# Part of V in the Q/K padding, interleaved early loads and a 256-token first chunk in a four-layer attention/GLU kernel

## The chip, the cores and the metric

The kernel runs on one core of one Trainium2 chip. The metric is the device time of one execution in microseconds (us). The fast runs of one kernel spread by up to 1.5%; a run is called fast or slow by comparison with the others of the same kernel. All comparisons below are between fast runs. "Span" is the length of the profiled execution; it is about 1.8 us shorter than the time given for that same execution.

Names of engines: PE is TensorE (matmul), PEld its weight load, DVE is VectorE, ACT is ScalarE, POOL is GpSimd, SP is SyncE, which here only issues DMAs.

## The reference, cut to what matters

```python
# S = 2048 tokens, D = 448, H = 16 heads of Dh = 28, F = 1792, bf16
def _A_ref(x, wqkv, wo):                 # attention: 8 keys at distances 0, 2, ..., 14
    qkv = (x @ wqkv).reshape(B, S, 3, H, Dh) ...
    logits = einsum(q, gathered k) * Dh ** -0.5    # masked, softmax over the 8 keys
    return einsum(attn, gathered v).reshape(B, S, D) @ wo

def _B_ref(x, w_gate, w_up, w_down):     # bilinear feed-forward
    return ((x @ w_gate) * (x @ w_up)) @ w_down

x = x + _A_ref(_layernorm(x), A_wqkv, A_wo)
x = x + _B_ref(_layernorm(x), B_w_gate, B_w_up, B_w_down)
x = x + _A_ref(_layernorm(x), ...)       # the same weights again
x = x + _B_ref(_layernorm(x), ...)
```

The four layers are numbered 0 to 3. Layers 0 and 2 are attention, 1 and 3 feed-forward.

## The kernel before: the parts that matter

A list scheduler, run in Python while the kernel is built, puts every operation into a fixed order on each engine. Layers overlap by chunks of 512 tokens. In attention, a head of 28 columns is stored in a slot of 32, so that Q and K carry four unused columns for each head.

Layernorm output is transposed before it feeds the matmuls. In layer 0 that is done on PE for the chunks in `PE_T`, and by a DMA transpose issued from SP for the rest. One chunk is four blocks of 128 tokens, so PE transposes blocks 0 to 11 and DMA blocks 12 to 15:

```python
PE_T = ("00","01","02")
# ... (in the layernorm of chunk j of layer li)
if not by_pe:
    sc.add("sp", one(lambda E, ...: E.dma_start_transpose(X[:, :, c0:c0 + 128], xn_sb[:, slot, 0:128 * nt]), ("T", li, B)), ...)
else:
    ... # E.transpose on PE into PSUM, then a copy by ACT or DVE
```

The loads: x and the V weights are issued from SP and the Q/K weights from ACT. The feed-forward weights are issued from ACT, one DMA each, only after the last quarter of x has landed. Gate weights go to partitions 0 to 63 and up weights to 64 to 127, because each pair of 64-row matmuls takes one operand half from each; the two run at the same time (fourteen of 512 columns, 376 ns each in the trace, take 1.69 us together). Down weights go to all 128 partitions:

```python
GATE = [("x", -1, 15)] if "02" in PE_T else [("xn", 0, 11)]
for nm, lo, src in (("wg", 0, B_w_gate), ("wu", 64, B_w_up)):
    plain_dma("act", WGU[lo:lo + 64, :, :], src.rearrange("(k p) f -> p k f", p=64), nm, f"d_{nm}", deps=GATE, ...)
plain_dma("act", WD[:], B_w_down.rearrange("(c p) e -> p c e", p=128), "wd", "d_wd", deps=GATE, ...)
```

The V matmuls of a pair of query blocks are 448 columns wide (the query blocks are 120 tokens, in groups of two):

```python
nv = D // 2 if split else D
def rhs(which, dc, lo, hi):
    return WV[lo:hi, dc, nv * which:nv * which + nv] if split else WV[lo:hi, dc, :]
```

The softmax here doesn't subtract the row's maximum and nothing guards it: scores larger than these inputs give would overflow.

Of the kernel before, what the change touches and what calls it, by code (L numbers as in the profile page):

```python
# [5 lines left out]
dt = mybir.dt  # L6
# [3 lines left out]
S = 2048  # L10
# [17 lines left out]
PE_T = ("00","01","02")  # L28
HEAD_LN = 4
HEAD_P = (-30.0,-29.5,-19.3,-17.8)  # L30
HOLD_A = 0.0
HOLD_BA = 2000.0
HOLD_BB = 0.0
HOLD_N = 2
# [5 lines left out]
LN0 = (2,2)  # L40
LN1 = (2,2)
VFIRST = False
WARM = 18
FILL = 30
SEED = 0
JITTER = 0.0
ATT_P = 0.6
A_CAP = 6
B_CAP = 8
SEQ = "A00 A01 B10 A02 B11 A03 B12 A20 B13 A21 B30 A22 B31 A23 B32 B33".split()  # L50
# [30 lines left out]
class Sched:  # L81
# [13 lines left out]
    def add(self, engs, ins, est, deps=(), prio=0.0, mode=None, acquire=None, release=(), dma=None, lat=0.0, after=None, selfd=()):  # L95
# [7 lines left out]
        op.prio += JITTER * self.rng.random()  # L103
        self.ops.append(op)
# [37 lines left out]
    def pick_banks(self, req, now):  # L142
        ok = [self.holder[b] is None and self.free_at[b] + self.LAT <= now + 1e-6 for b in range(8)]
        if req.pair:
            pairs = [p for p in range(4) if ok[2 * p] and ok[2 * p + 1]]
            if len(pairs) < req.n // 2:
                return None
            pairs.sort(key=lambda p: max(self.free_at[2 * p], self.free_at[2 * p + 1]))
            got = []
            for p in pairs[:req.n // 2]:  # L150
                got += [2 * p, 2 * p + 1]
            return got
        cand = [b for b in range(8) if ok[b]]
        if len(cand) < req.n:
            return None
        cand.sort(key=lambda b: (ok[b ^ 1], self.free_at[b]))
        return cand[:req.n]

    def schedule(self):
        self.holder = [None] * 8  # L160
        self.free_at = [-1e9] * 8
        self.last_rel = [None] * 8
# [24 lines left out]
        while left:  # L187
            moved = False
            b_ready = any(o.acquire is not None and o.acquire.kind == 1 for o in pend["pe"])
            for e in self.ENGS:  # L190
# [11 lines left out]
                for *_, op in cands:  # L202
                    if op.acquire is not None:
# [5 lines left out]
                        cap = (A_CAP if b_ready else 8) if kind == 0 else (B_CAP if a_wait else 8)  # L209
# [159 lines left out]
def build(nc, A_x, A_wqkv, A_wo, B_w_gate, B_w_up, B_w_down, out):  # L369
# [11 lines left out]
    NXN, NV, NE, NR, NG = 6, 4, 3, 3, 4  # L381
# [14 lines left out]
    v_sb = sb([128, NV, 512], bf, "v_sb")  # L396
    E_sb = sb([128, NE, 4, EW], bf, "E_sb")
    R_sb = sb([128, NR, EW], dt.float32, "R_sb")
    g_sb = sb([128, NG, 512], bf, "g_sb")
    hT = sb([128, FC, 2, 512], bf, "hT")  # L400
    oT = sb([128, 4, HALF], bf, "oT")
    ones32 = sb([128, 32], bf, "ones32")
    MK = sb([128, 3, 128], bf, "MK")
    ident = sb([128, 128], bf, "ident")
    warm = sb([128, 256], bf, "warm")
# [5 lines left out]
    sem_names += [f"d_x{i}" for i in range(NCH)] + ["d_stg0", "d_stg1", "d_stg2", "d_stg3", "d_wv", "d_wo", "d_wg", "d_wu", "d_wd", "d_out", "d_out2"]  # L411
    sem_names += [f"d_t{p}_{j}" for p in range(2) for j in range(NCH)]
# [14 lines left out]
    def load_x(q):  # L427
        two, b0 = q // 2, 4 * (q % 2)
        plain_dma("sp", x_sb[:, 4 * q:4 * q + 4, :], x_par[two][:, b0:b0 + 4, :], [("x", -1, B) for B in range(4 * q, 4 * q + 4)],
                  f"d_x{q}", lat=3300.0 + 700.0 * q, prio=-50 + q)  # L430

    load_x(0)
    for c in range(4):
        plain_dma("sp", WV[:, c, :], A_wqkv[CH_ROWS[c]:CH_ROWS[c] + 128, 2 * D:3 * D], ("wv", c), "d_wv", lat=5000.0, prio=-49.9)
    for q in range(1, NCH):
        load_x(q)
    for c in range(4):
        plain_dma("act", stage[:, 2 * D * c:2 * D * (c + 1)], A_wqkv[CH_ROWS[c]:CH_ROWS[c] + 128, 0:2 * D], ("stg", c), f"d_stg{c}", lat=4300.0, prio=-60)
# [5 lines left out]
    memset("dve", warm[:], 0.0, "c_warm", 100)  # L444
# [5 lines left out]
    sc.add("pool", one(lambda E: E.memset(v_sb[:].rearrange("p s (h e) -> p (s h) e", e=32)[:, :, DH:32], 1.0), "c_v"), 400, prio=-40)  # L450
    memset("pool", MK[:], 1.0, "i_mk0", 300)
# [10 lines left out]
    for n in range(WARM + FILL):  # L462
        sc.add("pe", one(lambda E: E.matmul(ps[:, wb[0], 0:256], warm[:, 0:128], warm[:], start=True, stop=True), ("warm", n)), 214.0 if n < WARM else 109.0, deps=["c_warm"], mode="F",
# [9 lines left out]
    WQKR = [("wqk", c, w) for c in range(4) for w in range(2)]  # L473
    WVR = [("wv", c) for c in range(4)]
    for j in range(4):
        dst = wo_g[32 * j:32 * j + DH, :, :]
        src = A_wo.rearrange("(c j e) d -> j e c d", c=4, j=4, e=DH)[j]
        plain_dma("sp", dst, src, ("wo", j), "d_wo", deps=["c_wo"], lat=12000.0, prio=-45)
    GATE = [("x", -1, 15)] if "02" in PE_T else [("xn", 0, 11)]
    for nm, lo, src in (("wg", 0, B_w_gate), ("wu", 64, B_w_up)):  # L480
        plain_dma("act", WGU[lo:lo + 64, :, :], src.rearrange("(k p) f -> p k f", p=64), nm, f"d_{nm}", deps=GATE, lat=12000.0 if lo == 0 else 20000.0, prio=-44)
    plain_dma("act", WD[:], B_w_down.rearrange("(c p) e -> p c e", p=128), "wd", "d_wd", deps=GATE, lat=26000.0, prio=-43)
    WO = [("wo", j) for j in range(4)]

    rings = {n: [None] * k for n, k in (("xn", NXN), ("v", NV), ("e", NE), ("r", NR), ("g", NG))}
# [17 lines left out]
    def ln_chunk(li, j, prio):  # L503
# [3 lines left out]
        groups = LN0 if li == 0 and j == 0 else LN1  # L507
        B0 = 4 * j
# [10 lines left out]
        for B in range(4 * j, 4 * j + 4):  # L519
# [6 lines left out]
            else:  # L526
                src = _twice_view(x_sb[:, B, :])
                dst = xn_sb[:, slot, :].rearrange("p (a t n) -> p a t n", a=7, t=2)
                c0 = 512 * (nbs[(li, j)] % 2) + 128 * (B % 4)
# [4 lines left out]
            if not by_pe:  # L534
                sc.add("sp", one(lambda E, slot=slot, c0=c0: E.dma_start_transpose(X[:, :, c0:c0 + 128], xn_sb[:, slot, 0:128 * nt]), ("T", li, B)),
                       1300.0, deps=[("xn", li, B)] + war, dma=f"d_t{par}_{j}", mode=li, lat=1400.0 if par == 0 else 1900.0, prio=prio)
# [18 lines left out]
    def crossed(parts, deps, prio, est, acquire):  # L555
        prev, prevk = None, []
        for n, (half, ins, pdeps) in enumerate(parts):
# [13 lines left out]
    def twin(u, tdeps, prio):  # L571
# [8 lines left out]
        crossed(parts, u["deps"] + tdeps, prio, pe_cols(u["n"]), u["bk"])  # L580

    def twin_blocks(outs, lhs, rhs, keys, groups, gdeps, deps, prio, acquire):
# [13 lines left out]
        crossed(parts, deps, prio, pe_cols(D), acquire)  # L596

    def qk_chunk(li, j, prio):
        X = xnT[0]
        c0 = 512 * j  # L600
        tdeps = [("T", li, B) for B in range(4 * j, 4 * j + 4)]
        war = []
        if li >= 2:
            lo, hi = 512 * j, 512 * (j + 1)
            for qb in range(NQB):
                k0, nk, tok, nq = qb_info(qb)
                if k0 < hi and tok + nq > lo:
                    war.append(("S", li - 2, qb))

        def unit(c):  # L610
            bk = Banks(2, pair=True)
            def out(which):
                return ps[:, bk[which], :]
            def lhs(which, dc, lo, hi):
                return WQK[lo:hi, dc, 1 - which, 128 * c:128 * c + 128]
            def rhs(which, dc, lo, hi):
                return X[lo:hi, dc, c0:c0 + 512]
            return dict(bk=bk, out=out, lhs=lhs, rhs=rhs, n=512, deps=WQKR, keys=(("Kps", li, j, c), ("Qps", li, j, c)), c=c)

# [3 lines left out]
        for u in us:  # L623
            bk, c = u["bk"], u["c"]
            def mk(eng, bk=bk, c=c):
                dst = qk[:, :, c, c0:c0 + 512]
                def fn(E):
                    src = ps[:, bk[0]:bk[0] + 2, :]
                    return E.activation(dst, src, ACT.Copy) if hasattr(E, "activation") else E.tensor_copy(dst, src)  # L629
                return fn  # L630
            sc.add(("act", "dve"), one(mk(None), ("QK", li, j, c)), {"act": act_est(1024), "dve": dve_est(1024)},
                   deps=[("Kps", li, j, c), ("Qps", li, j, c)] + war, release=[(bk, 0), (bk, 1)], prio=prio)
        for B in range(4 * j, 4 * j + 4):
            readersA.setdefault((li, B), []).extend([("Kps", li, j, 3), ("Qps", li, j, 3)])

    vslot = {}

    def v_group(li, qbs, prio):
# [15 lines left out]
        split = len(qbs) == 1  # L654
        nv = D // 2 if split else D
# [6 lines left out]
        def rhs(which, dc, lo, hi):  # L662
            return WV[lo:hi, dc, nv * which:nv * which + nv] if split else WV[lo:hi, dc, :]
        keys = tuple(("Vps", li, qbs[0], w) for w in range(2)) if split else tuple(("Vps", li, q) for q in qbs)
        twin(dict(bk=bk, out=out, lhs=lhs, rhs=rhs, n=nv, deps=WVR, keys=keys), tdeps, prio)
        n = len(qbs)
        s0 = slots[0][0]
        nk = infos[0][1]
        def fn(E):
# [3 lines left out]
            else:  # L673
                dst = v_sb[0:nk, s0:s0 + n, :].rearrange("p s (h e) -> p s h e", e=32)[:, :, :, 0:DH]
                src = ps[0:nk, bk[0]:bk[0] + n, 0:D].rearrange("p s (h e) -> p s h e", e=DH)
            return E.activation(dst, src, ACT.Copy) if hasattr(E, "activation") else E.tensor_copy(dst, src)  # L676
        sc.add(("act", "dve"), one(fn, [("V", li, q) for q in qbs]), {"act": act_est(n * D), "dve": dve_est(n * D)},
               deps=list(keys) + [p for _, p in slots] + ["c_v"], release=[(bk, 0), (bk, 1)], prio=prio)
# [3 lines left out]
    def attn_front(li, qb, prio):  # L682
# [3 lines left out]
        jl = ck // 512  # L686
        jh = (tok + nq - 1) // 512
        deps = [("QK", li, j, c) for j in range(jl, jh + 1) for c in range(4)]
# [25 lines left out]
    def attn_back(li, qb, slot, prio):  # L714
# [5 lines left out]
        for b in range(4):  # L720
            if not by_pe:
                break
            ins.append((lambda E, b=b: E.matmul(ps[32 * b:32 * b + 32, bk[1], 0:4 * nq], ones32[0:nk, :], E_sb[0:nk, slot, b, 0:4 * nq], start=True, stop=True, tile_position=(0, 32 * b)),
                        ("Dn", li, qb) if b == 3 else None))
        for h in range(H):
            b, hc = h % 4, h // 4
            ins.append((lambda E, b=b, hc=hc, h=h: E.matmul(ps[32 * b:32 * b + 32, bk[0], hc * nq:hc * nq + nq], v_sb[0:nk, vs, 32 * h:32 * h + 32],  # L727
                                                            E_sb[0:nk, slot, b, hc * nq:hc * nq + nq], start=True, stop=True, tile_position=(0, 32 * b)),
                        ("AV", li, qb) if h == H - 1 else None))
        sc.add("pe", ins, (200.0 if by_pe else 0.0) + 4 * 54.0, deps=[("E", li, qb, 0), ("E", li, qb, 1), ("V", li, qb), "c_ones", "c_v"], mode="C32", acquire=bk, prio=prio)  # L730
# [4 lines left out]
        else:  # L735
            sc.add("dve", one(lambda E: E.stream_shuffle(R_sb[:, rs, 0:4 * nq], ps[:, bk[0], 0:4 * nq], [DH] * 32), ("Rs", li, qb)), dve_est(4 * nq) + 100.0,  # L736
                   deps=[("AV", li, qb), prev], prio=prio)
# [5 lines left out]
        for B in range(tok // 128, (tok + nq - 1) // 128 + 1):  # L743
            if B >= 8:
                war.append(("Y", li, B - 8))
            elif li >= 2:
                war.append(("Y", li - 2, B + 8))
        cut = [tok] + [HALF] * (tok < HALF < tok + nq) + [tok + nq]
        ins = []
        for a, z in zip(cut, cut[1:]):  # L750
            def fn(E, a=a, z=z):
                return E.tensor_tensor(oT[:, :, a % HALF:a % HALF + z - a], ps[:, bk[0], 0:4 * nq].rearrange("p (h n) -> p h n", h=4)[:, :, a - tok:z - tok],  # L752
                                       R_sb[:, rs, 0:4 * nq].rearrange("p (h n) -> p h n", h=4)[:, :, a - tok:z - tok], ALU.mult)
            ins.append((fn, ("N", li, qb) if z == cut[-1] else None))
        sc.add("dve", ins, dve_est(4 * nq, fixed=70.0 * len(ins)), deps=[("AV", li, qb), ("R", li, qb)] + war, release=[(bk, 0)], prio=prio)
# [23 lines left out]
    def b_chunk(li, j, n_b, prio):  # L779
# [3 lines left out]
        tdeps = [("T", li, B) for B in range(4 * j, 4 * j + 4)]  # L783

        def unit(fc):
            acq = Banks(2, kind=1)
            def out(which):
                return ps[:, acq[which], :]
# [164 lines left out]
```

## Time and profile before

| | before |
|---|---|
| time, median of 4 | 409.46 us (three runs at 409.09 to 409.69; the fourth, 423.57, was slow and is not used) |
| span of the profiled run | 409.2 us (an execution of about 411.0 us, so slower than the median) |
| PE / DVE / ACT busy | 97% / 69% / 51% |
| first Q/K matmul, first gate/up matmul | 10.86 us, 68.74 us |
| PE work ordered before the first gate/up matmul (worked out as said below) | 43.1 us |

The first part of the page gives each engine's busy time, share of the span and number of instructions:

```profile
PE 395.4 (97%) x4606; PEld 191.3 (47%) x4606; DVE 281.8 (69%) x556; ACT 210.5 (51%) x356; POOL 11.9 (3%) x23
```

97% on PE looks as if only less matmul work could help. But busy is not the same as useful. A pair of 64-row matmuls takes columns/2.4 plus about 2.6 ns, by the starts in the timeline (from one group's start to the next, four pairs of 224 columns take 0.38 us at 111.81 us and seven pairs of 512 take 1.51 us at 87.36 us); summed over the instruction order that makes 367.5 us. The other 42 us lie mostly before 100 us. The table of busy time by stretch shows where (columns: the stretch, busy us and instruction count of each engine, granted PE clock, share of the 16 DMA engines, GB/s; a share over 1 means overlapping packets):

```profile
core 0: us, PE busy (x) PEld busy (x) DVE busy (x) ACT busy (x) POOL busy (x), PEclk, DMA share, GB/s
10.00:20.00 10.00, 7.86 (x64) 3.81 (x64) 7.14 (x22) 3.93 (x10) 0.00 (x0) 0.84 0.96 214
20.00:30.00 10.00, 9.70 (x122) 4.34 (x120) 7.92 (x19) 8.36 (x16) 2.12 (x1) 0.99 1.04 200
30.00:40.00 10.00, 8.97 (x154) 4.04 (x154) 7.29 (x14) 9.08 (x15) 2.09 (x1) 1.00 1.27 206
40.00:50.00 10.00, 8.83 (x126) 3.96 (x124) 9.52 (x16) 5.73 (x9) 2.00 (x1) 1.00 0.01 2
60.00:80.00 20.00, 17.48 (x216) 7.43 (x216) 17.12 (x36) 12.45 (x24) 0.00 (x0) 0.91 0.26 42
```

PE has holes and a lowered clock in 10 to 20 us and 60 to 80 us. And the DMA engines are full from 10 to 40 us at only about 200 GB/s: that is the feed-forward weights. The first hole has its origin on ACT. This is ACT's timeline (start, us, instruction, and in brackets the idle time before it):

```profile
12.23 0.70 ACTq L422 DMA_DIRECT2D WGU<-in_B_w_gate_dram  x1
12.96 1.51 ACTq L422 DMA_DIRECT2D WGU<-in_B_w_up_dram  x1
14.51 0.68 ACTq L422 DMA_DIRECT2D WD<-in_B_w_down_dram  x1
15.23 0.30 ACT L514 ACTIVATE lnv<-mv,eps_sb 128x2 f32<-128x2 f32 x1 [4.68 <-issue]
```

ACT's queue stands at the weight DMAs until x has landed (12.2 us), then spends 3 us issuing them. The layernorm step behind them finds ACT idle for 4.68 us; its own input from DVE was done at about 12.45 us, so the step comes some 2.8 us late. PE pays in its timeline:

```profile
10.86 3.85 PE L578 MATMUL ps<-xnTa,WQK 64*128 64x512 bf16 x34
16.82 1.01 PE L541 MATMUL ps<-ident,xn_sb 128*128 128x128 bf16 x8 [2.12 <-DVE mv L513]
17.76 2.90 PE L578 MATMUL ps<-xnTa,WQK 64*128 64x512 bf16 x14
```

Fourteen matmuls then take 2.90 us, where at full clock fourteen of the same take 1.69: the granted clock was 0.50 from 17 to 20 us.

The V group and the four DMA transposes of layer 0, in SP's timeline, with the line that gives their time from issue to landing:

```profile
L578 PE MATMUL ps<-WV,xnTa 64*128 64x448 bf16 (+1 forms) x252 | 28.5, 351 | 0.7 <-ACT E_sb L703 0.4
...
30.20 8.54 SPq L535 DMA_TRANSPOSE xnTa<-xn_sb  x4
...
DMA to landing us min/median/max: 3.5/5.8/7.8
```

Transposes of the later layers mostly land in about 2.5 to 3 us.

### The profile page before, as it was taken

What the parts mean: (1) busy time and instruction counts of PE and PEld (TensorE: products, weight loads), DVE (VectorE), ACT (ScalarE), POOL (GpSimd) and SP (SyncE); (2) the same over time, 40 slices, a digit from 0 to 9 for tenths busy, and PEclk for the clock granted to TensorE, in tenths of its full rate; (3) what the DMA queues carried; (4) which work ended last, traced back from release to release, by engine and by line L of the source; (5) the groups of instructions that cost most, each with busy time, mean ns of one, the idle gap of its engine ahead of it and who ended that gap; (6) DMA issues with size and microseconds to landing.
All of it is one profiled execution on the core that took longest, in us unless ns stands there. A gap on an engine that the chain in (4) does not pass through costs nothing.

```text
span 409.2 us, 10575 instructions
## 1 busy us (share of the span) xinstructions
PE 395.4 (97%) x4606; PEld 191.3 (47%) x4606; DVE 281.8 (69%) x556; ACT 210.5 (51%) x356; POOL 11.9 (3%) x23
## 2 busy tenths in 40 slices
PE   8798897999999999999999999999999999999997
PEld 6344333444544454444544445444554444444444
DVE  5687987989597768966697778964789723433432
ACT  4488586575368554667536584344854321321420
POOL 5022100000000000000000000000000000000000
PEclk9899998999999999999999999999999999999999
DMA  8999112430231033200241002310232032001001
GB/s 283 208 203 186 25 24 46 37 56 9 40 72 27 2 47 47 53 2 0 48 68 32 0 4 46 72 26 2 47 39 55 2 72 67 2 2 45 2 2 45
DMA packets 49573, 20.90 MB, mean 51 GB/s; under 512 B 41400, under 2 KB 48632, under 8 KB 49528
## 3 DMA queue, kind: packets, MB, share of 16 engines
q1 hardware_dynamic: 46072, 14.44, 19.1%
q10 hardware_dynamic: 3456, 5.79, 6.1%
q8 instruction: 36, 0.59, 0.6%
q14 instruction: 9, 0.07, 0.1%
HBM read 8.43 MB, written 1.84 MB: 25 GB/s over the span
## 4 chain that ended last, share of the span: by engine, by line
PE 89%; DVE 4%; ACT 2%; DMA 2%; SPq 1%; issue 1%; ACTq 1%
PE ps L797 41%; PE ps L594 25%; PE ps L578 16%; PE ps L727 2%; PE ps L696 2%; DMA x_sb<-in_A_x_dram 2%; PE ps L818 1%; DVE E_sb L709 1%; DVE qk L629 1%; ACT E_sb L703 1%; SPq L422 1%; ACTq L422 1%; DVE hT L806 1%; DVE x_sb L770 1%; PE ps L541 1%
## 5 line engine op out<-in xcount | busy, mean ns | idle before, releaser
L797 PE MATMUL ps<-xnTb,WGU 64*128 64x512 bf16 x1568 | 176.2, 376 | 1.6 <-DVE hT L806 0.4
L803 ACT ACTIVATE g_sb<-ps 128x512 bf16<-128x512 f32 x112 | 66.7, 598 | 108.4 <-PE ps L797 107.4
L797 PEld LDWEIGHTS ps<-xnTb,WGU 64*128 64x128 bf16 x1568 | 76.4, 94 | 89.6 <-issue 3.0
L806 DVE TENSOR_TENSOR hT<-g_sb,ps 128x512 bf16<-128x512 bf16 x112 | 75.6, 682 | 43.1 <-ACT g_sb L803 42.0
L594 PE MATMUL ps<-WD,hT 64*128 64x448 bf16 x840 | 85.0, 349 | 0.9 <-DVE hT L806 0.6
L703 ACT ACTIVATE E_sb<-ps 128x960 bf16<-128x960 f32 (+1 forms) x68 | 63.8, 972 | 16.0 <-PE ps L696 15.1
L594 PEld LDWEIGHTS ps<-WD,hT 64*128 64x128 bf16 x840 | 41.2, 94 | 38.7 <-DVE hT L806 1.2
L770 DVE TENSOR_TENSOR x_sb<-x_sb,ps 128x448 bf16<-128x448 bf16 x62 | 35.9, 614 | 33.5 <-PE ps L594 33.2
L578 PE MATMUL ps<-xnTa,WQK 64*128 64x512 bf16 x448 | 54.8, 383 | 0.4 <-ACT v_sb L676 0.2
L709 DVE TENSOR_TENSOR E_sb<-E_sb,MK 128x960 bf16<-128x960 bf16 (+1 forms) x65 | 43.5, 679 | 12.0 <-ACT E_sb L703 11.2
L511 DVE BATCH_NORM_STATS2 st<-x_sb 128x6 f32<-128x448 bf16 x64 | 37.2, 613 | 3.2 <-DMA x_sb<-in_A_x_dram 3.1
L532 DVE TENSOR_SCALAR xn_sb<-x_sb,mv,rstd 128x512 bf16<-128x512 bf16 (+1 forms) x64 | 34.1, 573 | 3.1 <-ACT rstd L516 2.9
L578 PEld LDWEIGHTS ps<-xnTa,WQK 64*128 64x128 bf16 x448 | 20.9, 95 | 26.4 <-issue 1.6
L629 ACT ACTIVATE qk<-ps 128x1024 bf16<-128x1024 f32 x22 | 22.4, 1023 | 20.7 <-PE ps L578 20.6
L594 PE MATMUL ps<-wo_g,oT 64*128 64x448 bf16 x256 | 29.7, 350 | 0.2
L578 PE MATMUL ps<-WV,xnTa 64*128 64x448 bf16 (+1 forms) x252 | 28.5, 351 | 0.7 <-ACT E_sb L703 0.4
L752 DVE TENSOR_TENSOR oT<-ps,R_sb 128x480 bf16<-128x480 f32 (+3 forms) x36 | 22.3, 625 | 4.1 <-ACT R_sb L740 3.8
L738 ACT ACTIVATE R_sb<-R_sb 128x480 f32<-128x480 f32 (+1 forms) x30 | 18.0, 600 | 13.4 <-DVE R_sb L736 13.3
L740 ACT ACTIVATE R_sb<-R_sb 128x480 f32<-128x480 f32 (+1 forms) x34 | 20.6, 606 | 0.3
L736 DVE STREAM_SHUFFLE R_sb<-ps 128x480 f32<-128x480 f32 (+1 forms) x30 | 20.6, 694 | 0.0
L629 DVE CAST qk<-ps 128x1024 bf16<-128x1024 f32 x10 | 12.2, 1225 | 9.3 <-PE ps L578 9.3
L594 PEld LDWEIGHTS ps<-wo_g,oT 64*128 64x128 bf16 x256 | 12.3, 95 | 12.5 <-PE ps L594 1.1
(47 smaller groups left out, 156.3 us busy)
## 6 DMA issues: line engine op xcount, KB each, us to landing
x_sb<-in_A_x_dram SPq DMA_DIRECT2D x4, 448.0 KB, 6.5
out_dram<-x_sb SPq DMA_DIRECT2D x15, 112.0 KB, 1.7
WGU<-in_B_w_gate_dram ACTq DMA_DIRECT2D x1, 1568.0 KB, 11.0
WGU<-in_B_w_up_dram ACTq DMA_DIRECT2D x1, 1568.0 KB, 18.2
WD<-in_B_w_down_dram ACTq DMA_DIRECT2D x1, 1568.0 KB, 22.8
hT<-in_A_wqkv_dram ACTq DMA_DIRECT2D x4, 224.0 KB, 4.9
xnTb<-xn_sb SPq DMA_TRANSPOSE x32, 3.0
WV<-in_A_wqkv_dram SPq DMA_DIRECT2D x4, 112.0 KB, 5.4
```

What stands on the lines that cost most here:

```text
L511: sc.add("dve", one(lambda E, B=B: E.bn_stats(st6[:, B, :], x_sb[:, B, :]), ("bn", li, B)), 525.0, deps=[("x", li - 1, B)] + ([("xn", li - ...
L532: sc.add("dve", one(lambda E, B=B, dst=dst, src=src: E.tensor_scalar(dst, src, mv[:, B, 0:1], rstd[:, B:B + 1], ALU.subtract, ALU.mult), ( ...
L578: parts[0 if s < 3 else 1][1].append((lambda E, w=w, c=c, lo=lo, st=st, sp_=sp_: E.matmul(u["out"](w), u["lhs"](w, c, lo, lo + 64), u["rhs ...
L594: ins.append((lambda E, w=w, c=c, lo=lo, st=st, sp_=sp_: E.matmul(outs(w), lhs(w, c, lo), rhs(w, c, lo), start=st, stop=sp_), keys[w] if s ...
L629: return E.activation(dst, src, ACT.Copy) if hasattr(E, "activation") else E.tensor_copy(dst, src)
L703: return E.activation(E_sb[0:nk, slot, 2 * hp:2 * hp + 2, 0:4 * nq], ps[0:nk, b0:b0 + 2, 0:4 * nq], ACT.Exp, scale=SCALE)
L709: return E.tensor_tensor(e, e, m, ALU.mult)
L752: return E.tensor_tensor(oT[:, :, a % HALF:a % HALF + z - a], ps[:, bk[0], 0:4 * nq].rearrange("p (h n) -> p h n", h=4)[:, :, a - tok:z - ...
L770: sc.add("dve", one(lambda E: E.tensor_tensor(x_sb[:, B, :], x_sb[:, B, :], ps[:, bk[w], 0:D], ALU.add), ("x", li, B)), dve_est(D), deps=[ ...
L797: ins.append((lambda E, u=u, k=k, w=w: E.matmul(u["out"](w), WGU[64 * w:64 * w + 64, k, 128 * u["fc"]:128 * u["fc"] + 128], X[64 * w:64 * ...
L803: sc.add("act", one(lambda E, gs=gs, bk=bk: E.activation(g_sb[:, gs, :], ps[:, bk[0], :], ACT.Copy), ("G", li, j, fc)), act_est(512), deps ...
L806: sc.add("dve", one(lambda E, gs=gs, bk=bk, fc=fc: E.tensor_tensor(hT[:, fc, hs, :], g_sb[:, gs, :], ps[:, bk[1], :], ALU.mult), ("H", li, ...
```

## The change

The intent is to take work off PE and to shorten the start:

- V of 4 of the 16 heads is computed in the unused Q/K columns, stored to DRAM and brought back by DMA transposes. The V matmuls shrink from 448 to 336 columns, except for the first four query blocks of layer 0.
- x comes in halves and quarters, the Q/K weights are split over both queues, the gate weights come in four column pieces, two of them issued by ACT at the very start. Up weights go to SP, down weights to ACT in two pieces.
- The first chunk of tokens is 256 instead of 512 (chunks 256/512/512/512/256 in layers 0, 1 and 3).
- Attention output is copied out of PSUM before it is normalised (`AVC`). The scheduler's priorities are new.

The diff, cut to its core:

```diff
 PE_T = ('00', '01', '02')
+VT = 4
+AVC = True
+PLAIN = 4
+ACH = {0: (256, 512, 512, 512, 256), 2: (512, 512, 512, 512)}
+BCH = {1: (256, 512, 512, 512, 256), 3: (256, 512, 512, 512, 256)}
 ...
-GATE = [("x", -1, 15)] if "02" in PE_T else [("xn", 0, 11)]
-for nm, lo, src in (("wg", 0, B_w_gate), ("wu", 64, B_w_up)):
-    plain_dma("act", WGU[lo:lo + 64, :, :], ..., nm, f"d_{nm}", deps=GATE, ...)
-plain_dma("act", WD[:], ..., "wd", "d_wd", deps=GATE, ...)
+plain_dma("sp", WGU[64:128, :, :], B_w_up..., "wu", "d_wu", ...)
+for n in range(4):
+    plain_dma("act", WGU[0:64, :, f0:f1], B_w_gate[:, f0:f1]..., ("wg", n), f"d_wg{n}", deps=[("rstd", 0, 3)] * (n > 1), ...)
+for n in range(2):
+    plain_dma("act", WD[:, 7 * n:7 * n + 7, :], ..., ("wd", n), f"d_wd{n}", deps=[("rstd", 0, 7)], ...)
 ...
+# after each Q/K chunk: 7 small stores of the padding columns to DRAM ("PW");
+# for each query block: sc.add("sp", ... dma_start_transpose(v2_sb[:, slot, :], vt_dram[li][:, k0:k0 + 128]) ("VT")
 ...
-nv = D // 2 if split else D
+nv = VD // 2 if split else D if plain else VD      # VD = 448 - 4 * 28 = 336
```

`PE_T` has not changed, but its chunks have. Three chunks now cover blocks 0 to 9 instead of 0 to 11.

## The prediction

> **What bounds the kernel.** TensorE (PE). The page gives PE 97% busy, DVE 69%, ACT 51%; the chain that ended last is 89% PE. From matmul starts in the timeline a pair of 64-row matmuls costs columns/2.4 + about 2.6 ns (eight 224-column ones take 0.38 us, so the slope holds). Summing the instruction order so gives 367.5 us of pure matmul work in 409.2 us. The other 42 us: nothing useful before the first transpose at 9.0 us (8.1 busy us there are warm-up), about 10 us of idle PE after it, nearly all before 70 us (2.1 at 15-17, 1.0 at 33, 1.2 at 43-44, 2.0 at 62-64), about 3.4 us lost at half clock (granted clock 0.50 in 17-20 us and around 65-68 us, each just after an idle stretch), 2.4 us after the last matmul, and the rest is 123 changes of array tiling at about 0.13 us. [...]
>
> **What the change does.**
> 1. V of 4 of 16 heads rides in the Q/K padding: V matmuls shrink from 448 to 336 columns for 30 of 34 query blocks. 105 pairs x 112/2.4 ns = 4.9 us less PE work, all critical. Price: 56 small DMAs to DRAM and 30 DMA transposes back, on SP. Transposes now land 2.5-3.0 us after issue, out-stores 1.7 us, so this V should come 7-10 us after its Q/K copy; mostly hidden.
> 2. Head. x in halves, Q/K weights split over both queues, 256-token first chunk. The last Q/K weight still lands near 8 us, but two blocks need less layernorm. First Q/K matmul about 9 us instead of 10.9. The gate-weight DMAs no longer sit in the middle of ACT's stream: now they hold ACT from 10.6 to 15.2 us, starve the layernorm and cause both the 2.1 us hole and the half clock after it. Worth 4-5 us.
> 3. First gate/up matmuls move from 43 us to 37 us of preceding PE work, filling holes where DVE (about 80-95% busy before 70 us) is the limit: 1-3 us.
> 4. Costs: AV copies out of PSUM, 30 x about 0.55 us on ACT/DVE, off the chain but releasing banks sooner; 256-column chunks +0.6 us PE; 6 more tiling changes +0.8 us; last chunk's final H awaited by all remaining matmuls, +0.8 us.
>
> Sum: 409.5 - 4.9 - 0.4 (fewer transposes) + 2.2 - 6.5 = about 400.
>
> **Prediction: 400 us, 8 in 10 between 395 and 405.5.** Faster by over 2%: 0.63; within 2%: 0.36; slower: 0.01.
>
> **What would show it.** V matmul group: busy 28.5 to about 23 us, 336-column pairs near 143 ns. First Q/K matmul at or before 9.5 us. PE idle between 9 and 70 us down from about 9 to under 5 us, no 0.50 clock at 17-20 us. First gate/up matmul at 50-56 us, not 68.7. Waits of the AV matmuls on v transposes under 1 us in total. DVE busy about 290, ACT about 220 us. After 100 us, PE idle stays about 2.5 us.
>
> **What would make it wrong.** Weights queued on SP ahead of transposes could delay the first DMA transposes to 35 us and stall the fourth chunk; gate pieces loaded early may delay x and starve the layernorm; the DRAM round trip may be longer than planned, holding AV and in-order SP behind it; new idle gaps may drop the clock again at another place.

The sum comes to 409.5 - 4.9 - 0.4 + 2.2 - 6.5 = 399.9, about 400 us; the 3.4 us at half clock are read from the trace (a mean clock of 0.992 over 409.2 us makes 3.3 us). The 0.13 us for a change of array tiling is an estimate, since the prediction puts down to 123 changes what is left of the 42 us. In the timeline of the kernel before a change adds about 0.10 us: seven pairs of 512 columns take 1.61 us with a change behind them (81.19 to 82.80 us) and 1.51 us without (87.36 to 88.87 us).

## The result, and the profile after

| | before | after |
|---|---|---|
| time, median of 4 | 409.46 us | 405.78 us (405.61 to 406.66) |
| ratio, 95% interval | | 0.9896 (0.9865 to 0.9926): the same within 2% |
| span of the profiled run | 409.2 us | 404.0 us |
| first Q/K matmul | 10.86 us | 10.83 us |
| first gate/up matmul | 68.74 us | 60.61 us |
| PE work ordered before it | 43.1 us | 36.7 us |
| time not covered by PE work, first 100 us | 27.3 us | 26.4 us |

Ratios here and below are the mean time of one kernel's fast runs over that of the other's of the same rounds, so they are not quite the ratio of the medians that are quoted. Where I turn a ratio into us, I multiply by 410 us. The last two rows are worked out as before, from columns and instruction order. The profiled run of the kernel before was slower than its median, so the spans (5.2 us apart) show more than the medians (3.7 us).

PE is less busy, by 7 us, and the V group shrank as planned. But the first gate/up matmul came 8.1 us earlier with 6.4 us less PE work ahead of it, so the start itself gained hardly 2 us, and over the first 100 us only 1 us. First the busy line and the V group of the kernel after:

```profile
PE 388.4 (96%) x5046; PEld 211.9 (52%) x5046; DVE 293.1 (73%) x602; ACT 222.6 (55%) x406; POOL 15.8 (4%) x29
...
L650 PE MATMUL ps<-WV,xnTa 64*128 64x336 bf16 (+2 forms) x252 | 22.8, 301 | 0.1
```

The waits of PE in the first 100 us (releaser, us in total, times, longest):

```profile
PE ps L650 <- DMA xnTa<-xn_sb: 4.7, 1, 4.7
PE ps L612 <- DVE xn_sb L603: 2.6, 2, 1.6
PE ps L907 <- DVE R_sb L842: 1.2, 1, 1.2
```

The longest is new, a wait on a DMA transpose. Here it is in PE's timeline, with SP's two groups of transposes and the time to landing below:

```profile
34.40 1.69 PE L650 MATMUL ps<-xnTa,WQK 64*128 64x512 bf16 x14
40.82 1.47 PE L650 MATMUL ps<-xnTa,WQK 64*128 64x512 bf16 x6 [4.73 <-DMA xnTa<-xn_sb]
...
26.45 8.12 SPq L606 DMA_TRANSPOSE xnTa<-xn_sb  x4
35.15 4.39 SPq L606 DMA_TRANSPOSE xnTa<-xn_sb  x2
...
DMA to landing us min/median/max: 3.9/8.9/12.0
```

The stretches, to be set against those of before:

```profile
10.00:20.00 10.00, 8.29 (x123) 5.13 (x122) 7.65 (x26) 7.11 (x15) 1.21 (x6) 1.00 1.13 266
20.00:30.00 10.00, 9.91 (x144) 4.72 (x140) 9.44 (x24) 8.65 (x19) 4.28 (x2) 1.00 1.07 222
30.00:40.00 10.00, 6.08 (x82) 2.43 (x76) 7.83 (x7) 5.67 (x8) 4.00 (x2) 0.95 1.22 202
40.00:50.00 10.00, 9.18 (x98) 3.99 (x100) 3.54 (x5) 3.77 (x6) 0.00 (x0) 0.70 0.27 49
50.00:60.00 10.00, 9.46 (x180) 5.44 (x176) 9.24 (x19) 7.33 (x12) 0.00 (x0) 1.00 0.48 57
60.00:80.00 20.00, 19.10 (x334) 14.64 (x336) 18.45 (x43) 14.79 (x34) 0.00 (x0) 1.00 0.23 46
```

The hole and the half clock have moved from 15 to 20 us and 62 to 68 us, to 36 to 46 us. PE shows 9.18 busy in 40 to 50 us, but at a mean clock of 0.70. The pieces of the chain that ended last, in order of time, name the two early limits:

```profile
2.81 9.32 DMA x_sb<-in_A_x_dram
...
32.81 7.88 DMA xnTa<-xn_sb
```

The quarters of x needed 9.3, 11.5 and 13.8 us from issue to landing, where before they needed at most 7.8, because gate pieces were now in flight beside them (e6, below, moves only the feed-forward weights, and x needs 5.2 to 6.5 us again). And the fourth transpose, issued at 32.81 us, landed only 7.88 us later.

The stretch at half clock (0.50 to 0.52 in 40 to 46 us) comes behind a hole of 4.73 us. In the kernel before the clock fell to 0.50 behind holes of only 2.12 us (at 15 us) and 1.98 us (at 62 us), while b1, below, went on at a clock of 1.00 behind one of 1.97 us (at 58.5 us). So a hole of about 2 us was followed by half clock in some places and not in others; how long a hole has to be is not shown.

**The theories.** Theory A: the up weights, now on SP ahead of the transposes, hold them up by their place in that queue. Theory B: any feed-forward weights in flight do so, in whichever queue, and the start can't become shorter before they have landed. Theory C: the start is limited by DVE, so that removing the stall gives nothing. In e6's text the letters differ: its Theory C is that the gate pieces take bandwidth from x, and its Theory D is the Theory C given here. After e6, B was sharpened to B′: the whole stretch up to 40 us is bounded by the bulk weights, and the remedy is not to move but to delay those that aren't needed.

### The profile page after: what moved, and what is told of

Same layout as the page of the kernel before. It is cut to its first block, busy times and chain, and to the rows that moved or that the text cites. A ratio compares the mean times of both kernels' runs of the same rounds, so it can differ in the third digit from the quotient of the medians.

```text
span 404.0 us, 11727 instructions
## 1 busy us (share of the span) xinstructions
PE 388.4 (96%) x5046; PEld 211.9 (52%) x5046; DVE 293.1 (73%) x602; ACT 222.6 (55%) x406; POOL 15.8 (4%) x29
## 4 chain that ended last, share of the span: by engine, by line
PE 87%; DMA 5%; DVE 5%; ACT 1%; issue 1%; SPq 0%
PE ps L907 41%; PE ps L666 25%; PE ps L650 14%; DMA xnTa<-xn_sb 3%; DMA x_sb<-in_A_x_dram 2%; PE ps L826 2%; PE ps L793 2%; PE ps L928 1%; DVE st L582 1%; DVE E_sb L806 1%; ACT E_sb L800 1%; DVE x_sb L878 1%; DVE hT L916 1%; DVE qk L702 0%; PE ps L612 0%
## 5 line engine op out<-in xcount | busy, mean ns | idle before, releaser
L907 PE MATMUL ps<-xnTb,WGU 64*128 64x512 bf16 (+1 forms) x1960 | 179.4, 333 | 2.5 <-DVE R_sb L842 1.2
L907 PEld LDWEIGHTS ps<-xnTb,WGU 64*128 64x128 bf16 x1960 | 96.6, 94 | 73.6 <-issue 2.8
L913 ACT ACTIVATE g_sb<-ps 128x512 bf16<-128x512 f32 (+1 forms) x140 | 71.2, 513 | 92.7 <-PE ps L907 91.8
L916 DVE TENSOR_TENSOR hT<-g_sb,ps 128x512 bf16<-128x512 bf16 (+1 forms) x140 | 78.9, 575 | 44.8 <-ACT g_sb L913 42.1
L650 PE MATMUL ps<-xnTa,WQK 64*128 64x512 bf16 (+1 forms) x504 | 55.0, 362 | 5.6 <-DMA xnTa<-xn_sb 5.4
L702 ACT ACTIVATE qk<-ps 128x1024 bf16<-128x1024 f32 (+1 forms) x22 | 19.6, 906 | 16.3 <-PE ps L650 16.2
L702 DVE CAST qk<-ps 128x1024 bf16<-128x1024 f32 (+1 forms) x14 | 16.0, 1142 | 11.4 <-PE ps L650 11.3
L844 ACT ACTIVATE R_sb<-R_sb 128x480 f32<-128x480 f32 (+1 forms) x30 | 18.0, 604 | 10.2 <-DVE R_sb L842 9.8
L650 PE MATMUL ps<-WV,xnTa 64*128 64x336 bf16 (+2 forms) x252 | 22.8, 301 | 0.1
L860 DVE TENSOR_TENSOR oT<-O_sb,R_sb 128x480 bf16<-128x480 f32 (+3 forms) x32 | 19.5, 614 | 2.6 <-ACT R_sb L846 2.5
L842 DVE STREAM_SHUFFLE R_sb<-O_sb 128x480 f32<-128x480 f32 (+1 forms) x30 | 20.5, 689 | 0.0
## 6 DMA issues: line engine op xcount, KB each, us to landing
WGU<-in_B_w_gate_dram ACTq DMA_DIRECT2D x4, 392.0 KB, 10.3
WD<-in_B_w_down_dram ACTq DMA_DIRECT2D x2, 784.0 KB, 19.8
x_sb<-in_A_x_dram SPq DMA_DIRECT2D x3, 448.0 KB, 11.5
```

Source lines behind the costliest of these rows:

```text
L650: parts[0 if s < 3 else 1][1].append((lambda E, w=w, c=c, lo=lo, st=st, sp_=sp_: E.matmul(u["out"](w), u["lhs"](w, c, lo, lo + 64), u["rhs ...
L702: return E.activation(dst, src, ACT.Copy) if hasattr(E, "activation") else E.tensor_copy(dst, src)
L842: sc.add("dve", one(lambda E: E.stream_shuffle(R_sb[:, rs, 0:4 * nq], osrc(), [DH] * 32), ("Rs", li, qb)), dve_est(4 * nq) + 100.0, deps=[ ...
L907: ins.append((lambda E, u=u, k=k, w=w: E.matmul(u["out"](w), WGU[64 * w:64 * w + 64, k, 128 * u["fc"]:128 * u["fc"] + 128], X[64 * w:64 * ...
L913: sc.add("act", one(lambda E, gs=gs, bk=bk: E.activation(g_sb[:, gs, 0:nt], ps[:, bk[0], 0:nt], ACT.Copy), ("G", li, j, fc)), act_est(nt), ...
L916: sc.add("dve", one(lambda E, gs=gs, bk=bk, fc=fc: E.tensor_tensor(hT[:, fc, hs, 0:nt], g_sb[:, gs, 0:nt], ps[:, bk[1], 0:nt], ALU.mult), ...
```

## The experiments

Twelve runs, all with correct results. The schedule was kept (of the changed kernel, in b1 and b2 of the kernel before): after scheduling, a DMA was taken from one queue and inserted in the same or another at a given place, and nothing else was moved on PE, DVE and POOL. e4, e5 and e12 add PE work in the kept order instead (e12 on top of e9); only e8 and e10 were scheduled anew. "Before" is the kernel before in the same rounds.

| run | time, median (range), us | before | ratio (95%) |
|---|---|---|---|
| e1_wu_act | 405.25 (404.69 to 406.27) | 409.75 | 0.9905 (0.9864 to 0.9946) |
| e3_wu_wd_late | 404.76 (403.32 to 405.62) | 409.75 | 0.9880 (0.9829 to 0.9931) |
| e4_fill | 404.33 (404.23 to 404.51) | 409.75 | 0.9880 (0.9843 to 0.9917) |
| e5_vfull | 409.04 (408.75 to 410.61) | 409.75 | 1.0002 (0.9960 to 1.0044) |
| e6_swap | 403.82 (403.23 to 404.50) | 410.98 | 0.9841 (0.9797 to 0.9885) |
| b1_loads_sp | 407.24 (405.84 to 407.48) | 410.98 | 0.9926 (0.9876 to 0.9976) |
| e9_wd_late | 398.01 (395.50 to 401.29) | 409.81 | 0.9692 (0.9616 to 0.9769) |
| e8_pe_t | 401.52 (401.04 to 402.72) | 409.81 | 0.9778 (0.9721 to 0.9835) |
| e10_both | 401.64 (400.67 to 404.85) | 409.81 | 0.9802 (0.9725 to 0.9879) |
| e11_wd_only | 401.57 (400.70 to 403.02) | 410.99 | 0.9776 (0.9735 to 0.9818) |
| e12_vfull9 | 401.55 (400.48 to 402.80) | 410.99 | 0.9779 (0.9730 to 0.9829) |
| b2_wd_late | 407.33 (405.85 to 407.87) | 410.99 | 0.9907 (0.9867 to 0.9948) |

### e1: the up weights from the other queue

```diff
+move("wu", "act", ("wd", 1), False)     # from SP to ACT, behind the second down piece
```

> The changed kernel with one load moved: the 1568 KB up-weight load is issued from ACT's queue, right after the second piece of the down weights, instead of from SP's queue ahead of the first DMA transposes. The order of instructions on every compute engine is frozen as it was. Theory A (ring order: the six transposes of tokens 1280 to 2047 stand behind the up weights in SP's queue): transposes land in 6 us or less instead of a median of 8.9, the fourth by 36.5 us instead of 40.7, the PE gap at 36 to 41 us falls from 4.7 to under 1.5 us, the half clock after it goes, time 398 to 400. Theory B (all 16 DMA engines are full with weights until 38 us, whichever queue they come from): transposes land at 38 us or later as before, time 403.5 to 406.

The time did not change beyond the spread: 405.25 against 405.78 us. PE's timeline still has the stall:

```profile
41.48 1.05 PE L650 MATMUL ps<-xnTa,WQK 64*128 64x512 bf16 x6 [3.51 <-DMA xnTa<-xn_sb]
```

Transposes still needed up to 9.2 us, although nothing bulky was left ahead of them in SP's queue. Theory A falls as the main cause. Here are the packets and MB of ACT's queue (q10) and SP's (q1) from 33 to 35 us, and of SP's from 38 to 39 us, after the up weights had landed:

```profile
q10 hardware_dynamic: 103, 0.35, 92.4%
q1 hardware_dynamic: 84, 0.02, 37.6%
...
q1 hardware_dynamic: 1057, 0.25, 131.0%
```

The transposes' packets are small (about 240 bytes each: 0.25 MB in 1057) and those of the weights about 3.4 KB (0.35 MB in 103). While the other queue had weights to move, the two queues passed almost as many packets, 84 against 103 in 2 us; afterwards SP's alone passed 1057 in 1 us. Not explained is that none of SP's packets ran from 29.2 us, the issue of the first transpose, to 33 us.

### e3: up and down weights issued at 35.6 to 37.7 us

```diff
+for k in ("wu", ("wd", 0), ("wd", 1)):
+    move(k, "act", ("Rl", 0, 2), True)
```

> The changed kernel, order of the compute engines frozen; up and down weights are both issued from ACT just before the Ln of query block 2 (about 36 to 43 us), so that the six transposes meet nearly idle DMA engines. A and B both expect the gap to go: transposes land 2.5 to 4 us after issue, no idle PE at 36 to 41 us, clock 1.0 throughout 20 to 60 us, time 397 to 400. If the transposes are late for another reason (SP issues them late, their source comes late from DVE), the gap stays above 3 us and the time above 403.

Min, median and max over the six transposes of layer 0:

```profile
DMA to landing us min/median/max: 2.5/2.5/11.8
```

The first four, issued at 28.4 to 32.4 us, now landed in 2.5 us, the fifth (34.2 us) in 4.1, and the stall at 36 us was gone, so weights in flight are the cause of the late landing. The sixth, issued at 35.4 us as the weights started, took 11.8 us. But the time was 404.76 us, not the 397 to 400 that both theories expected. The load of 3.2 MB was now in flight from 36 us on, when the padding's stores, V's transposes and the next layer's transposes need the DMA engines. V's first transpose took 5.4 us (2.6 in the changed kernel) and landed at 53.83 us, and the matmuls that use V started at 53.92. The first gate/up matmul came at 58.08 us, with 2.4 us of waiting just before and a clock of 0.82 in 50 to 60 us. The cost was moved, not removed.

### e4: the stall filled with dummy matmuls

```diff
+# 40 matmuls of 256 columns on zeros, after the wait for PSUM and before the wait for the transpose
+sc.filler = {hold.idx: ("d_t0_3", lambda E: [E.matmul(ps[:, hb, 0:256], warm[:, 0:128], warm, start=True, stop=True) for _ in range(40)])}
```

> The changed kernel with 40 dummy matmuls of 256 columns (about 4.4 us at full clock) put on PE after the matmuls that come before the gap at 36 us and before the wait for the transposes, into the PSUM bank that the waiting group overwrites; all else is as it was. The gap stays as long, but PE is active in it. If the stretch at half clock (39.3 to about 46 us) is caused by the idle gap and costs what the clock record says, 6.6 us at half speed, the time falls by 2.5 to 3.5 us to about 402.5 to 403.2. If the half clock costs nothing on the chain, it stays at 405.5 to 406.

The hole is filled and the six matmuls behind it run at full clock (0.82 us instead of 1.47):

```profile
37.92 4.54 PE L1009 MATMUL ps<-hT 128*128 128x256 bf16 x40
42.40 0.82 PE L656 MATMUL ps<-xnTa,WQK 64*128 64x512 bf16 x6
```

The time fell by 1.5 us by the medians (405.78 to 404.33) and by 0.7 us by the ratios, less than the 2.5 to 3.5 us expected. But this is not the price of the half clock alone. In e4's profiled run another stretch of lowered clock came earlier (mean clock 0.88 in 10 to 20 us and 0.95 in 20 to 30 us, behind a hole of 1.91 us at 14 us), and the six matmuls started 1.6 us later than in the changed kernel (42.40 against 40.82 us). From them to the first gate/up matmul it took 16.4 us instead of 19.8 (58.84 less 42.40, and 60.61 less 40.82), so 3.4 us were gained there. How much of that the half clock alone costs at the end stays open.

For the kernel before, the record has a hint. Its 28 fast runs in the experiments' rounds fall into groups by mean clock: 407.6 and 407.8 us at 1.000, 408.6 to 409.9 us at 0.996 (14 runs), 411.0 to 412.8 us at 0.992 (11 runs), 413.5 us at 0.988. A step of 0.004 is 1.6 us of lost clock in 408 us, about one stretch like that of 17 to 20 us in the profile above, and it goes with about 2 us of time. So most of the spread between the runs of this kernel goes with the mean clock; that it is the number of such stretches is an estimate from these figures. This is read from the list of runs; no experiment set the clock alone.

### e5 and e12: V at full width again

```diff
-            return ps[:, bk[which], 0:nv]
+            return ps[:, bk[which], 0:nf]              # nf = 448 or 224; the extra columns are not used
-            return WV[lo:hi, dc, nv * which:nv * which + nv] if split else WV[lo:hi, dc, 0:nv]
+            return WV[lo:hi, dc, nv * which:nv * which + nf] if split else WV[lo:hi, dc, 0:nf]
```

On the changed kernel:

> The changed kernel with the V matmuls back at 448 (and 224) columns for all query blocks; the extra columns are computed and not used, the evacuation and the route through DRAM stay. Orders frozen. If the 4.9 us of PE work that the shorter V matmuls save are on the critical path, the time rises by 3.5 to 5 us to 409 to 411. If they were mostly saved in stretches where PE waits for DVE, ACT or DMA anyway, it rises by under 2 us.

It lost 3.3 us by the medians (409.04 less 405.78), 4.3 us by the ratios (1.0002 less 0.9896). With V at full width the changed kernel was as slow as the kernel before: everything else in the change came to nothing. The same edit on the best version, e9:

> e9_wd_late with the V matmuls back at 448 and 224 columns (the extra columns are computed and not used): the worth of the V cut where nothing early absorbs it. If the V term of 4.9 us is all critical: e9 + 4.5 to 5.2 us, 402.5-403.5 us. If part of it is covered (as the 3.3 us measured on the changed kernel suggests): e9 + 2.5 to 4 us.

It lost 3.5 us by the medians and 3.6 us by the ratios. The V cut is worth 3.3 to 4.3 us of the 4.9 us less PE work. The two profiled runs differ by 5.3 us in span (399.0 against 393.7), but the latter was the fastest of its kernel's four, so this isn't used.

### e6: gate and up weights swapped between the queues

```diff
+for n in (3, 2, 1, 0):
+    move(("wg", n), "sp", ("wo", 3), False)   # gate pieces behind x on SP
+move("wu", "act", ("wd", 0), True)            # up weights on ACT, at 13.8 us
```

> The changed kernel, compute orders frozen, with the two weight streams swapped: the four gate pieces are issued from SP after all of x and wo (where the up weights stood), the up weights from ACT just before the down weights (about 15 us); so no feed-forward weight is in flight before all of x has been queued. Theory C (the gate pieces that are loaded from 2 us on take half the DMA bandwidth from x; x quarters 2, 3, 4 land at 12.1, 17.7, 21.4 us instead of at most 10.6 and 12.2 before the change, and layernorm, transposes and PE follow): x lands by about 9.5, 12 and 14 us, the PE gap at 14 to 15.6 us goes, the first DMA transpose is issued by 24.5 us, the gap at 36 us shrinks to under 1.5 us, time 397 to 401. Theory D (DVE and ACT are the limit of the first 60 us, x's landing does not matter): x lands as early, but the first gate/up matmul stays at 59 to 61 us and the time at 404 to 406.

The start became what the change had intended: all of x had landed by 12.4 us (12.2 before the change), the first Q/K matmul started at 9.94 us, the hole at 14 us was gone (PE busy 9.58 and 10.00 in 10 to 20 and 20 to 30 us). But the stall at 36 us did not shrink below 1.5 us as expected, and the first gate/up matmul came at 59.89 us, which is what the rival (its Theory D) expected; e9 decides between the two. The time fell by only 2 us, to 403.82, because PE reached the same wall earlier:

```profile
32.08 1.69 PE L650 MATMUL ps<-xnTa,WQK 64*128 64x512 bf16 x14
40.22 1.46 PE L650 MATMUL ps<-xnTa,WQK 64*128 64x512 bf16 x6 [6.46 <-DMA xnTa<-xn_sb]
...
DMA to landing us min/median/max: 6.5/10.3/12.8
```

The transposes were issued 2.3 us earlier than in the changed kernel (24.13 against 26.45 us), but the matmul that waits for them started only 0.6 us earlier. It starts when the bulk ends (the last down weights land at 39.73 us), not when the transposes are issued.

### b1 and b2: the kernel before, with the loads moved

b1 issues gate, up and down weights from SP behind x, so that ACT doesn't stand at them. b2 in addition delays the down weights to just before the first gate copy.

```diff
+for k in ("wd", "wu", "wg"):                  # b1
+    move(k, "sp", ("wo", 3), False)
---
+for k in ("wu", "wg"):                        # b2
+    move(k, "sp", ("wo", 3), False)
+move("wd", "act", ("G", 1, 0, 0), True)
```

> The kernel before, compute orders frozen, with one part of the change alone: gate, up and down weights are issued from SP's queue after wo instead of from ACT's, still after the wait for the last quarter of x. ACT is then not held from 10.6 to 15.2 us. My prediction's reason (this hold causes the 2.1 us hole at 15 us and the half clock after it): hole and half clock at 17 to 20 us go, time falls by 3 to 4 us to 405.5 to 406.5. If the ramp is limited elsewhere (DVE/ACT work before 70 us), the hole goes but under 1.5 us is left of it at the end: 408 to 409.5.

> The kernel before with gate and up loads issued from SP after x (as b1_loads_sp) and the down load from ACT just before the first gate copy. Before does blocks 0 to 11 of the first layer by PE transposes and needs its DMA transposes only at 43-47 us, so theory B' says that the end of the bulk doesn't bound it: 405.5-408 us, within 1.5 us of b1_loads_sp (407.2). If late down weights help any version alike: 401-403 us.

b1 removed the hole at 15 us and, in its profiled run, both stretches of half clock; it gained 3.0 us by the ratio (3.7 by the medians), as expected. Its stretch from 10 to 20 us, where the kernel before has PE busy for 7.86 us at a clock of 0.84:

```profile
10.00:20.00 10.00, 9.98 (x102) 5.04 (x100) 9.44 (x27) 6.81 (x16) 0.00 (x0) 1.00 0.93 209
```

The profiled run was the fastest of the four (405.84 us, mean clock 1.000). The other three had a mean clock of 0.996 and took 407.2 to 407.5 us, about 2 us less than the runs of the kernel before with that clock. So the prediction's reading of the first hole was right, and a line's move in the kernel before would have mended it. b2 was no better than b1 (407.33 and 407.24 us): in the old schedule PE transposes twelve blocks itself and the end of the bulk bounds nothing.

### e9 and e11: the down weights when they are needed

e9 is e6 with one more move; e11 makes this move alone. In the changed kernel the down weights are first needed at 77.7 us, but they are in flight from 17 to 40 us. In e9 they are issued at 51.8 us, land at most 8.5 us later and are first needed at 67.7 us.

```diff
+for k in (("wd", 0), ("wd", 1)):
+    move(k, "act", ("G", 1, 0, 0), True)      # just before the first gate copy
```

> As e6_swap, but the two down-weight pieces (1.6 MB) are issued from ACT just before the first gate copy, near 60 us; they are needed near 77 us. Theory B' (the first 40 us are bounded by bulk weights on the 16 DMA engines; transposes land only when the bulk ends): bulk ends near 28-30 us instead of 38, the six transposes land by 32-34 us, the PE stall of 6.5 us before 40 us shrinks below 1.5 us, no half clock after it, time 397-400.5 us. Rival C (transposes are slow for their own sake, or the early work is bounded elsewhere, by DVE): stall over 3 us, or stall gone and time still 402.5 us or more.

> The changed kernel with only the two down-weight pieces moved to just before the first gate copy (gate pieces stay on ACT, up on SP ahead of x). Fills the two-by-two of e6_swap (only the swap: 403.8) and e9_wd_late (both: 398.0). Theory B': with the bulk ending near 30 us the transposes issued at 26-33 us land in about 3 us, the stall of 4.7 us at 36 us and the half clock after it go; the hole at 14 us stays; 399-402 us. Rival (both parts needed, since x's third and fourth quarters land late at 18-21 us here): 403-405 us.

e9 took 398.01 us, 11.8 us less than before by the medians and 7.8 us less than the change (8.4 us by the ratios to before; the experiments' rounds ran on four different chips). Its PE and DVE orders are those of the changed kernel, instruction for instruction. Its stretches:

```profile
10.00:20.00 10.00, 9.82 (x146) 5.38 (x142) 9.47 (x31) 8.46 (x17) 3.25 (x6) 1.00 1.14 234
20.00:30.00 10.00, 10.00 (x146) 5.02 (x146) 8.34 (x20) 8.49 (x20) 2.00 (x1) 1.00 1.14 212
30.00:40.00 10.00, 10.00 (x142) 4.71 (x140) 9.58 (x9) 7.37 (x10) 4.01 (x2) 1.00 0.57 87
40.00:50.00 10.00, 9.47 (x180) 5.44 (x176) 9.24 (x19) 8.34 (x14) 0.00 (x0) 1.00 0.48 62
50.00:60.00 10.00, 9.39 (x174) 7.61 (x176) 8.68 (x20) 7.55 (x17) 0.00 (x0) 1.00 0.69 188
```

The last bulk load now lands at about 30.5 us (the up weights, 16.8 us after their issue at 13.68) instead of 35 to 40 us, and the clock is 1.00 throughout. The transposes, their landing and the first gate/up matmul:

```profile
23.74 6.69 SPq L606 DMA_TRANSPOSE xnTa<-xn_sb  x4
31.00 3.41 SPq L606 DMA_TRANSPOSE xnTa<-xn_sb  x2
...
DMA to landing us min/median/max: 3.4/4.9/7.3
...
50.37 0.94 PE L907 MATMUL ps<-xnTb,WGU 64*128 64x256 bf16 x14 [0.90 <-DVE R_sb L842]
```

No PE wait on a transpose of layer 0 is left. The first gate/up matmul comes 10.2 us earlier than after the change, and the span is 10.3 us shorter: the whole gain of the start is kept to the end. (This profiled run is the fastest of four; by the medians the gain is 7.8 us.)

With e11 the two moves make a two-by-two. In ratios to before: neither 0.9896, swap alone 0.9841, down weights alone 0.9776, both 0.9692. So the swap is worth 2.3 us alone, the late down weights 4.9 us alone, both 8.4 us. They add up to within the noise: the intervals of these ratios are 0.3 to 0.8% to either side, 1 to 3 us. In e11, x still lands late and PE still has holes between 10 and 30 us (busy 7.55 and 8.11 of 10), mostly on the layernorm:

```profile
PE ps L612 <- DVE xn_sb L603: 4.0, 4, 1.7
```

Its transposes land in 2.5 to 4.1 us and the stall is gone. Its rival expectation, that both parts are needed, falls; so does Theory C, by e9.

### e8 and e10: all transposes of layer 0 on PE

```diff
-PE_T = ('00', '01', '02')
+PE_T = ('00', '01', '02', '03', '04')         # on e6 (e8), on e9 (e10); scheduled anew
```

> As e6_swap, but all transposes of layer 0 are done on PE (chunks 3 and 4 too: blocks 10 to 15), so that no DMA transpose has to pass the weight loads; PE pays 24 more 128-column transposes, about 1.4 us, and DVE/ACT 6 more copies out of PSUM. The scheduler recomputes the order. Theory B': stall before 40 us gone, no half clock there, first gate/up matmul below 58 us, time 397-401 us. Rival C (early work is bounded by DVE anyway): the PE gap is spread over 30-60 us in small waits on DVE and the time stays 402.5-405 us.

> e8_pe_t and e9_wd_late together. Theory B': no better than the better of the two (both remove the same wait), within 1 us. Rival C: no expectation of gain beyond e6_swap.

e8 took 401.52 us, a shade outside its range: 2.3 us better than e6. The stall and the half clock are gone, with the weights arriving as early as in e6. This is a second way to remove the wait, and it supports that the wait was the cost, though with another order throughout. e10 was no better than e8 (401.64), which fits that both remove the same wait, but it missed its expectation to be as good as e9. What the remaining 3.5 us between e8 and e9 consist of is open. PE does 24 more transposes (1.4 us by the expectation's estimate; in the kernel before eight of them take 0.62 us at 20.59 us, the last one's own 0.22 us included, so one starts every 57 ns or so), and the scheduler produced another order throughout, so the two can't be told apart.

## Why the prediction was wrong

It said 400 us, and the change gave 405.78. Term by term:

1. **V cut, "4.9 us less PE work, all critical": the mechanism was right, the size somewhat too large.** The group went from 28.5 to 22.8 us of busy time. Taking the cut back cost 3.3 to 4.3 us (e5) and 3.5 us (e12). AV waits on V's transposes after the DRAM round trip did not show up, as predicted.
2. **"Head … Worth 4-5 us": this step failed.** The reading of the old hole was right (b1: 3.0 to 3.7 us, by moving the loads off ACT). But the first Q/K matmul didn't start at 9 us but at 10.83. The first two pieces of x were not late (they landed at 4.26 and 5.50 us; in e6 at 4.46 and 5.81). The last Q/K weights were: they landed at 8.83 us, in e6, with no gate pieces beside them, at 6.83. DVE stood at copying them before it could go on with the layernorm:

```profile
8.85 0.28 DVE L523 COPY WQK<-hT 128x448 bf16<-128x448 bf16 x1 [1.25 <-DMA hT<-in_A_wqkv_dram]
```

e6 restored 9.94 us. And the whole gain was given back at 36 us, as a stall of 4.73 us and a stretch at half clock.
3. **"First gate/up matmuls move … filling holes: 1-3 us": failed for the same reason.** The matmul came at 60.61 us, not at 50 to 56. In e9 it came at 50.37 us with the same PE order. So the change does contain this gain; the DMA traffic hid it.
4. **Costs, +2.2 us: not measured one by one.** The time not covered by PE work after 100 us rose by 0.5 us (14.5 to 15.0), which is no contradiction.

In the sum, the term of 6.5 us for head and filling measured about 1 us (27.3 to 26.4 us of uncovered time in the first 100 us). The prediction took the landing time of transposes, 2.5 to 3.0 us, from stretches without bulk loads, although the kernel before showed 3.5 to 7.8 us under load in layer 0. And it didn't ask when the transposed blocks are needed in the new order: at 36 us, inside the bulk that ends at 38 to 40 us, instead of at 47 us, well after it. It named the right symptom among its risks ("could delay the first DMA transposes to 35 us and stall the fourth chunk"), but with a cause that e1 refuted, the place in SP's queue. It is the load in flight on the DMA engines that counts.

Why the bulk is in flight so long can be read in part. Gate and up weights together are 3.2 MB and moved at about 200 GB/s (16 to 28 us); x, with the attention weights, moved at up to 390 GB/s (4 to 6 us) and down weights at about 340 (32 to 34 us), in the kernel before. Gate and up in flight together in e6 and e9 moved 184 to 212 GB/s between 13 and 22 us as well. Why these two are slower is not shown, since no experiment changed their transfers. At the 340 GB/s of the down weights they would need about 9.5 instead of 16 us (an estimate from these rates).

## What to carry to other kernels

Before shortening a start, list what each DMA is needed for and when, and delay the bulk whose need is latest: here the down weights, needed at 77.7 us, stood in the way of transposes needed at 36 us, and moving them was worth 4.9 us by the ratios (6.1 once the gate and up weights were swapped), against 3.3 to 4.3 us for the V cut. When chunk sizes change, check which blocks change sides between PE and DMA transposes, and take the landing time of small DMAs from a stretch with the same traffic. And when a hole is removed, ask what the engine runs into next; a second hole may be waiting at a fixed time.
